# Top-32 attention with a following MLP: the selection of the limit for six row blocks at once, masks ten row blocks behind the scores

## The chip, the core and the metric

The kernel runs on one core of a Trainium2 chip. The metric is the device time of one launch in microseconds (us). A core has five engines with a queue each, which work through their own instructions in order and wait for one another by semaphores: PE (TensorE, matrix products), ACT (ScalarE), DVE (VectorE), POOL (GpSimd) and SP (SyncE, which issues most of the DMAs here).

## The reference

Attention over 64 heads (8 batches of 8), each with 576 rows of 64 numbers; of each row's 576 scores only those count that reach the 32nd largest. Then an MLP with a leaky ReLU over all 4608 tokens.

```python
scores = scale * np.matmul(q, k.transpose(0, 1, 3, 2))
kth = np.partition(scores, -top_k, axis=-1)[..., -top_k:-top_k + 1]
scores = np.where(scores >= kth, scores, -1000000000.0)
attn = np.exp(scores - np.max(scores, axis=-1, keepdims=True))
attn = attn / (np.sum(attn, axis=-1, keepdims=True) + 1e-09)
attn_out = np.matmul(attn, v)
# x: attn_out as 4608 tokens of 512
h = x @ w_in
out = (np.maximum(h, 0.0) + alpha * np.minimum(h, 0.0)) @ w_out
```

## The kernel before

**Row blocks.** Two heads make a pair; there are 32 pairs with nine row blocks (128 rows of one head, or the last 64 rows of both) each, 288 in all. `ORDER` lists them: pair after pair for the first 252, and mixed across the four pairs of the last batch for the last 36, so that its tokens become complete one group after another. One pass of the main loop (line 765) is a **tick**; in tick `n` the row block `n` gets its scores read, and older row blocks get their later steps. The order of instructions within each engine is written out by hand (`manual_schedule`), so the program's order is the engines' order.

**One row block's way.** PE computes the scores into PSUM (`scores`, line 326), one or two row blocks ahead. ACT copies them to `b` while adding `NT0`, the negative of an estimate of the row's limit (`act_b`, line 335), and sums the signs of `b` (`act_s`, line 341), which tells how many scores lie above the estimate. POOL makes of it a sign word `SG` (`side_of`, line 351), DVE turns the bits of `b` so that the scores on the wanted side of the estimate are ordered (`flip`, line 357, output `y`). DVE then finds the eight largest of each of six segments (`seg_ops`, line 367) two ticks behind the scores and merges the 48 candidates to the 24 largest, `L` (`merge_ops`, lines 382 and 384), three ticks behind. The place of the limit in this list is known from the sum of signs:

- `sel_a` (ACT, line 390): `ra = (S + 513)^2`
- `sel_eq` (DVE, line 395): `EQ` is one where `ra` equals an entry of the table `iota`, 24 entries per row block
- `sel_pr` (DVE, line 401): `L = EQ * L`
- `sel_sum` (DVE, line 405): the sum over the 24 entries, into `KK`
- `limit` (DVE, line 411): `KP`, the limit with its bits turned back

These five run once for three row blocks. Seven ticks behind the scores DVE compares `b` with the limit (`mask`, line 431, output `mk`), and POOL multiplies the mask with the exponentials (`weights`, line 441, output `w`). For the last six row blocks one fused DVE operation does both (line 438). The exponentials `e` come from ACT (`act_e`, line 346). SP transposes `w` by DMA (lines 449 to 454), and `tail_of` enters what follows in a calendar by ticks: the product with V on PE three or four ticks later (`av`, line 489; `av_last` for the last batch), the normalisation on DVE and ACT, the transposed tokens (`x_turn`), and the MLP's steps (`feed`).

**Units.** ACT handles `b` and `e` in units of one or two row blocks (`unit_of`). Row blocks 0 to 7 of a pair are four units of two; row block 8 is a unit by itself. A unit of two has five buffers for `b` and four for `e`, a unit of one has one of each. `act_e` comes in the tick of the unit's last row block.

**Prologue of a pair.** `prep_plan` prepares each pair (transposes of q and k, and the estimate `NT0` from a few statistics) in steps at fixed ticks relative to `BASE[p]`. `load` and `load_v` issue the loads of q, k and V some 18 and 13 ticks ahead of it; V lands in one of two buffers `st_v` and is copied to bf16 by ACT (`act_v`, line 201). From pair 12 on, and again from pair 21 on, the preparation runs one pair further ahead; the pairs 11 and 20 are prepared four ticks early for this.

**The MLP between.** The steps of the MLP (`ph_step`, line 644, with the ReLU `gT` on ACT, line 650; `pz_step`, lines 658 and 662, with a copy on ACT, line 667) and first the preparation of its weights (lines 556 to 620) wait in the queue `back`. Each tick has a credit of 1.9 (2.4 after the last scores), each step a price (0.9 for `ph`, 1.5 for `pz`). Up to tick 253 a tick takes one step at most, later as many as the credit allows with two banks at most.

**Order on DVE in a tick:** masks due, the sum of the selection held over from the tick before, the segments and merges interleaved, calendar steps `dve`, `limit`, `sel_eq`, `flip`, calendar steps `dvx`, `sel_pr`. On POOL: the products, then `SG`. On ACT: the ReLUs left from the tick before, `act_b` if a unit begins, calendar steps, `act_s`, `act_e` if a unit ends, `sel_a`.

Of the kernel before, what the change touches and what calls it, by code (L numbers as in the profile page):

```python
# [16 lines left out]
S = 576  # L17
NSEG = 6
SEG = S // NSEG
KW = 24  # L20
# [12 lines left out]
def kernel(  # L33
# [75 lines left out]
    st_vs = [prep.tile([128, 10, D], FP32, name=f"st_v{i}", bufs=1) for i in range(2)]  # L109
# [5 lines left out]
    def early_sets():  # L115
# [4 lines left out]
        for t_ in st_vs:  # L120
            nc.vector.memset(t_[64:128, 4, :], 0.0)
            nc.vector.memset(t_[0:64, 5, :], 0.0)
# [9 lines left out]
    def load(p, eng2=None):  # L132
# [10 lines left out]
        pairs[p] = dict(q=st_q, k=st_k, st_v=st_vs[p % 2], v=v_bfs[p % NV])  # L143

    def load_v(p):
        hA = 2 * p
        st_v = st_vs[p % 2]
# [14 lines left out]
    while n < NT:  # L162
        m = 1 if ORDER[n][1] == 8 and ORDER[n + 1][1] != 8 else 2
        for i in range(m):
            unit_of[n + i] = (n, m, i)
        units.append((n, m))
        n += m
    LEAD1, LEAD2 = 11, 20
    BASE = {p: TPP * (p - (p > LEAD1) - (p > LEAD2)) for p in range(NPAIR)}
    BASE[LEAD1] -= 4  # L170
    BASE[LEAD2] -= 4

    def prep_plan(p):
# [26 lines left out]
        def act_v():  # L200
            nc.scalar.copy(d["v"][:, :, 0:D], d["st_v"])
# [87 lines left out]
        if p == 1:  # L289
            ts = [-9, -8, -7, -6, -5, -4, -3, -2, -2, -2, -2, -2, -1, -1, 1]  # L290
        else:
            ts = [-14, -13, -12, -11, -10, -9, -7, -6, -5, -5, -4, -4, -3, -2, -8]
# [5 lines left out]
                 dict(dve=[dve_6]), dict(act=[act_v])]  # L298
# [29 lines left out]
    def act_b(n0):  # L328
        m = unit_of[n0][1]
        b = attn.tile([128, m, S], FP32, name=f"b{m}", bufs=5 if m == 2 else 1)  # L330
# [6 lines left out]
        tiles[n0]["bu"] = b  # L337
# [5 lines left out]
    def act_e(n0):  # L343
        m = unit_of[n0][1]
        e = attn.tile([128, m, S], BF16, name=f"e{m}", bufs=4 if m == 2 else 1)
        nc.scalar.activation(e, tiles[n0]["bu"], AF.Exp, scale=scl)  # L346
# [25 lines left out]

    def merge_ops(n):
        C = Cs[n // TPP][:, n % TPP, :, :].rearrange("p g e -> p (g e)")
        if n % 3 == 0:
            Ls[n // 3] = attn.tile([128, 3, KW], FP32, name="L", bufs=2)
        L = Ls[n // 3][:, n % 3, :]
# [10 lines left out]
    def sel_a(m):  # L388
        a = attn.tile([128, 3], FP32, name="ra", bufs=2)
        nc.scalar.activation(a, S_all[:, 3 * m:3 * m + 3], AF.Square, bias=c513)  # L390
        sel[m] = a

    def sel_eq(m):
        EQ = attn.tile([128, 3, KW], FP32, name="EQ", bufs=1)
        nc.vector.tensor_tensor(EQ, sel[m].unsqueeze(2).to_broadcast([128, 3, KW]),
                                iota.unsqueeze(1).to_broadcast([128, 3, KW]), ALU.is_equal)
        sel[m] = EQ

    def sel_pr(m):
        L = Ls.pop(m)  # L400
# [591 lines left out]
```

## Time and profile before

| | |
|---|---|
| median of three runs | 879.25 us |
| lowest and highest | 878.42 and 879.33 us |
| the profiled execution | 875.27 us |
| its span, first to last instruction | 873.2 us |
| mean granted TensorE clock | 0.919 |

The span is what the views below count from; the execution's own time is 2.1 us longer. A row of a group gives the line, the engine, the operation, output and inputs, the shapes, the count, the busy time in us, the mean duration in ns, and the idle time of the engine just ahead of it with what ended most of it. A row of the timeline gives start and duration in us. Durations of neighbours on an engine overlap in the records: the next instruction's start is earlier than the end of the one before. A row of a stretch gives the length and then the busy time of PE, PEld, DVE, ACT and POOL with counts, the granted clock, the DMA share and GB/s.

### The profile page before, as it was taken

The numbers are of one execution on the slowest core, as the hardware profiler recorded it, in microseconds if no ns is written. First come the engines' busy times: TensorE is split into PE (matmuls) and PEld (weight loads), VectorE is DVE, ScalarE is ACT, GpSimd is POOL, SyncE is SP. The second block draws the span as 40 slices with busy tenths as digits, with TensorE's granted clock in tenths as the row PEclk, the third lists the DMA queues.
The fourth block names the chain that finished last, engine by engine and source line by source line (L and its number), as shares of the span: only waits on it lengthen the run. The fifth ranks groups of instructions, "written<-read, shape, count | busy, mean of one in ns | idle before, by whom it ended". The sixth has DMA issues, their size and how long they took to land.

```text
span 873.2 us, 20627 instructions
## 1 busy us (share of the span) xinstructions
PE 725.9 (83%) x5747; PEld 426.9 (49%) x5747; DVE 833.7 (95%) x5185; ACT 789.7 (90%) x1873; POOL 430.1 (49%) x629
## 2 busy tenths in 40 slices
PE   6677687878968799878997789977897989899995
PEld 4344454434544355544454345634455555556663
DVE  4999999999999999999999999999999999999990
ACT  6999999899999999899998999999999999879851
POOL 1455455555545555545555554555554555555520
PEclk9666789699989999899987999999999999899998
DMA  7899644644666445555576456465456564355451
GB/s 163 154 180 204 122 96 92 128 95 88 147 129 116 90 109 120 114 117 95 118 159 116 83 104 132 104 129 101 101 118 123 112 101 100 80 96 101 81 99 41
DMA packets 343019, 99.50 MB, mean 114 GB/s; under 512 B 335200, under 2 KB 335216, under 8 KB 342896
## 3 DMA queue, kind: packets, MB, share of 16 engines
q1 hardware_dynamic: 340544, 95.71, 55.0%
q0 software_dynamic: 1152, 2.10, 1.9%
q8 instruction: 47, 0.77, 0.4%
q14 instruction: 76, 0.62, 0.3%
q10 hardware_dynamic: 1200, 0.30, 0.2%
HBM read 36.71 MB, written 9.44 MB: 53 GB/s over the span
## 4 chain that ended last, share of the span: by engine, by line
DVE 70%; ACT 13%; PE 12%; DMA 2%; issue 1%; POOL 1%; SPq 0%; DVEq 0%
DVE C L367 23%; DVE y L357 11%; DVE mk L431 10%; DVE C L384 9%; DVE L L382 8%; PE pz L662 3%; PE ps L326 3%; ACT b L335 3%; ACT h L341 3%; ACT e L346 2%; PE ph L644 2%; DVE P L244 2%; ACT gT L650 1%; DVE L L401 1%; DVE KK L405 1%
## 5 line engine op out<-in xcount | busy, mean ns | idle before, releaser
L441 POOL TENSOR_TENSOR w<-mk,e 128x576 bf16<-128x576 bf16 x250 | 318.9, 1276 | 336.5 <-DVE mk L431 183.9
L367 DVE MAX8 C<-y 128x8 f32<-128x96 f32 x1728 | 420.8, 244 | 0.1
L326 PE MATMUL ps<-qkT 64*128 64x288 f32 (+1 forms) x1280 | 253.8, 471 | 36.1 <-ACT b L335 35.9
L341 ACT ACTIVATE h<-b 128x576 bf16<-128x576 f32 x288 | 202.8, 704 | 1.6
L335 ACT ACTIVATE b<-ps,NT 128x576 f32<-128x576 f32 x288 | 202.0, 759 | 2.2 <-PE ps L326 2.1
L644 PE MATMUL ph<-xT,w_in_b 128*128 128x128 bf16 (+2 forms) x1088 | 158.5, 294 | 42.2 <-ACT gT L650 35.2
L326 PEld LDWEIGHTS ps<-qkT 64*128 64x128 f32 (+1 forms) x1280 | 133.6, 192 | 96.4 <-ACT b L335 60.1
L346 ACT ACTIVATE e<-b 128x1152 bf16<-128x1152 f32 (+1 forms) x158 | 174.1, 1102 | 0.0
L382 DVE MAX8 L<-C 128x8 f32<-128x48 f32 x864 | 163.5, 189 | 0.1
L357 DVE TENSOR_SCALAR y<-b,SG 128x576 int32<-128x576 int32 x288 | 147.1, 511 | 7.2 <-POOL SG L351 6.8
L431 DVE TENSOR_SCALAR mk<-b,KP 128x576 bf16<-128x576 f32 x282 | 143.8, 510 | 0.0
L644 PEld LDWEIGHTS <-w_in_b 128*128 128x128 bf16 x1088 | 85.7, 101 | 108.5 <-issue 80.0
L662 PE MATMUL pz<-w_out_b,gT 128*128 128x512 bf16 x576 | 138.6, 380 | 0.0
L650 ACT ACTIVATE gT<-ph 128x512 bf16<-128x512 f32 x144 | 88.0, 618 | 37.8 <-PE ph L644 37.6
L384 DVE MATCH_REPLACE8 C<-L,C 128x48 f32<-128x48 f32 x576 | 108.9, 189 | 0.0
L662 PEld LDWEIGHTS <-gT 128*128 128x128 bf16 x576 | 53.2, 98 | 70.6 <-issue 14.0
L489 PE MATMUL pu<-v_bf,wT 128*128 128x65 bf16 (+1 forms) x1600 | 69.6, 198 | 10.4 <-DMA wT<-w 6.8
L489 PEld LDWEIGHTS <-wT 128*128 128x128 bf16 (+1 forms) x1600 | 65.0, 103 | 21.4 <-DMA wT<-w 8.1
L351 POOL TENSOR_SCALAR SG<-S_all 128x1 int32<-128x1 f32 x288 | 64.6, 224 | 17.6 <-ACT h L341 17.5
L441 POOL TENSOR_TENSOR wm<-mk,e 128x576 bf16<-128x576 bf16 x32 | 40.8, 1275 | 49.9 <-DVE mk L431 47.1
L341 ACT ACTIVATION_READ_ACCUMULATOR h<-b 128x1 f32 x288 | 62.6, 217 | 0.0
L518 ACT ACTIVATE xb<-pu,rz 128x64 bf16<-128x64 f32 x224 | 54.3, 367 | 0.0
(100 smaller groups left out, 711.8 us busy)
## 6 DMA issues: line engine op xcount, KB each, us to landing
out_dram<-o_sb SPq DMA_DIRECT2D x35, 256.0 KB, 2.4
st_q<-in_q_dram SPq DMA_DIRECT2D x64, 128.0 KB, 2.9
st_v<-in_v_dram SPq DMA_DIRECT2D x64, 128.0 KB, 2.6
kst<-in_k_dram SPq DMA_DIRECT2D x62, 128.0 KB, 2.7
w_stage<-in_moe_w_out_dram SPq DMA_DIRECT2D x16, 256.0 KB, 3.1
w_in_b<-in_moe_w_in_dram POOLq DMA_DIRECT2D x8, 256.0 KB, 6.2
wT<-w SPq DMA_TRANSPOSE x128, 3.3
st_q<-in_q_dram SPq DMA_DIRECT2D x32, 32.0 KB, 2.7
```

The costliest lines, as they stand in the source:

```text
L326: nc.tensor.matmul(o_, l_, r_, start=True, stop=True)
L335: nc.scalar.activation(t["b"].rearrange("p (a c) -> p a c", a=2), t["ps"], AF.Identity, bias=NT0[:, p * TPP + j:p * TPP + j + 1], scale=ON ...
L341: nc.scalar.activation(h, tiles[n]["b"], AF.Sign, accum_out=S_all[:, n:n + 1])
L346: nc.scalar.activation(e, tiles[n0]["bu"], AF.Exp, scale=scl)
L357: nc.vector.tensor_scalar(t["y"].bitcast(I32), t["b"].bitcast(I32), FLIP, SG[:, n:n + 1], ALU.bitwise_xor, ALU.bitwise_xor)
L367: return [lambda g=g: nc.vector.max(out=C[:, n % TPP, g, :], in_=t["y"][:, g * SEG:(g + 1) * SEG]) for g in range(NSEG)]
L382: ops.append(lambda r=r, src=src: nc.vector.max(out=L[:, 8 * r:8 * r + 8], in_=src))
L384: ops.append(lambda r=r, src=src: nc.vector.match_replace(out=C2, in_to_replace=L[:, 8 * r:8 * r + 8], in_values=src, imm_value=NEG))
L431: nc.vector.tensor_scalar(t["mk"], t["b"], row_limit(n), None, ALU.is_ge)
L441: nc.gpsimd.tensor_tensor(dst, t["mk"], t["e"], ALU.mult)
L644: nc.tensor.matmul(hold[f][:, i, :], w_in_b[:, kk, (f + i) * 128:(f + i + 1) * 128], xT[:, kk, c0:c0 + tb], start=(kk == 0), stop=(kk == N ...
L662: nc.tensor.matmul(pz[0:m], hold["gT"][:, f, r0:r0 + m], w_out_b[:, f, :], start=False, stop=(f == NFT - 1))
```

## The change

- **Selection.** `GROUPS` forms groups of six for the first 252 row blocks and of three for the last 36. `sel_a`, `sel_eq`, `sel_pr`, `sel_sum` and `limit` run once for each group, their tiles are six wide.
- **Masks.** `mask` and `weights` of a row block come ten ticks behind its scores instead of seven; from row block 249 on this falls to seven, so that two row blocks fall due in each of the ticks 258, 259 and 260. Only the first of two gets a mask and the product on POOL; the second is done by the fused operation on DVE.
- **Exponentials.** `act_e` comes three ticks after its unit's last row block, two from row block 260 on, one from 268 on, none from 276 on.
- **Units.** Row blocks 0 to 7 are four units of two, row block 8 is a unit by itself, and from 9 on row blocks go two by two, across pairs; the last one is by itself. `b` has six buffers of two, `e` four of two.
- **Loads.** One buffer `st_v` instead of two; `load_v(1)` comes in tick 1, `act_v` of pair 1 in tick 5; `load_v(p)` not earlier than seven ticks ahead of `BASE[p - 1]`.
- **Preparation.** The pairs 11 and 20 are two ticks early instead of four, their followers two and one ticks late; `dve_6` moves to tick -3 behind `flip`.

```diff
-        m = 1 if ORDER[n][1] == 8 and ORDER[n + 1][1] != 8 else 2
+        m = 1 if n in (8, NT - 1) else 2
...
-    BASE[LEAD1] -= 4
-    BASE[LEAD2] -= 4
+    for p in (LEAD1, LEAD2):
+        for i, late in enumerate((-2, 2, 1)):
+            BASE[p + i] += late
...
-            ts = [-9, -8, -7, -6, -5, -4, -3, -2, -2, -2, -2, -2, -1, -1, 1]
+            ts = [-9, -8, -7, -6, -5, -4, -3, -2, -2, -2, -2, -2, -1, -1, -4]
         else:
-            ts = [-14, -13, -12, -11, -10, -9, -7, -6, -5, -5, -4, -4, -3, -2, -8]
+            ts = [-14, -13, -12, -11, -10, -9, -7, -6, -5, -5, -4, -4, -3, -3, -8]
...
-        b = attn.tile([128, m, S], FP32, name=f"b{m}", bufs=5 if m == 2 else 1)
+        b = attn.tile([128, 2, S], FP32, name="b", bufs=6)
...
-        e = attn.tile([128, m, S], BF16, name=f"e{m}", bufs=4 if m == 2 else 1)
-        nc.scalar.activation(e, tiles[n0]["bu"], AF.Exp, scale=scl)
+        e = attn.tile([128, 2, S], BF16, name="e", bufs=4)
+        nc.scalar.activation(e[:, 0:m, :], tiles[n0]["bu"], AF.Exp, scale=scl)
...
+    GROUPS = [(i, 6) for i in range(0, N0, 6)] + [(i, 3) for i in range(N0, NT, 3)]
+    group_of = {i: (g, z) for g, z in GROUPS for i in range(g, g + z)}
...
-    def sel_eq(m):
-        EQ = attn.tile([128, 3, KW], FP32, name="EQ", bufs=1)
-        nc.vector.tensor_tensor(EQ, sel[m].unsqueeze(2).to_broadcast([128, 3, KW]),
-                                iota.unsqueeze(1).to_broadcast([128, 3, KW]), ALU.is_equal)
-        sel[m] = EQ
+    def sel_eq(g, z):
+        EQ = attn.tile([128, 6, KW], FP32, name="EQ", bufs=1)[:, 0:z, :]
+        nc.vector.tensor_tensor(EQ, sel[g].unsqueeze(2).to_broadcast([128, z, KW]),
+                                iota.unsqueeze(1).to_broadcast([128, z, KW]), ALU.is_equal)
+        sel[g] = EQ
...
-            wdue.setdefault(wn + LAG_W if wn < NW else 3 * (wn // 3) + 7, []).append(wn)
+            g, z = group_of[wn]
+            at = wn + 10 - max(0, min(3, (wn - N0 + 5) // 2)) if wn < NW else g + 7
+            assert at >= g + z + 4
+            wdue.setdefault(at, []).append(wn)
+        edue = {}
+        for n0, m in units:
+            at = n0 + m - 1
+            edue.setdefault(at + (0 if at >= NT - 12 else 1 if at >= NT - 20
+                                  else 2 if at >= NT - 28 else 3), []).append(n0)
+        ga = {g + z: (g, z) for g, z in GROUPS}
+        gm = {g + z - 1: (g, z) for g, z in GROUPS}
...
+            if n == 1:
+                load_v(1)
...
-                if n == max(0, BASE[p] - 13):
+                if n == max(BASE[p] - 13, BASE[p - 1] - 7 + 4 * (p == 2)):
                     load_v(p)
...
-            if n >= 3 and n % 3 == 0 and n - 3 < NT:
-                sel_a((n - 3) // 3)
+            for n0 in edue.get(n, ()):
+                act_e(n0)
+            if n in ga:
+                sel_a(*ga[n])
...
-            for wn in due:
+            for wn in due[0:1]:
                 if wn < NW:
                     mask(wn)
...
-                weights(wn, wn >= NW)
+                weights(wn, wn >= NW or wn != due[0])
```

More of the change, by code (lines that the diff above doesn't have):

```diff
@@ L108 @@
     ksts = [prep.tile([128, 5, 130], FP32, name=f"kst{i}", bufs=1) for i in range(2)]
-    st_vs = [prep.tile([128, 10, D], FP32, name=f"st_v{i}", bufs=1) for i in range(2)]
+    st_v = prep.tile([128, 10, D], FP32, name="st_v", bufs=1)
     NV = 6
@@ L200, in act_v @@
         def act_v():
-            nc.scalar.copy(d["v"][:, :, 0:D], d["st_v"])
+            nc.scalar.copy(d["v"][:, :, 0:D], st_v)
         def pe_k():
@@ L297, in prep_plan @@
                  {dvx: [dve_3]}, dict(dve=[dve_4]), {dvx: [dve_4b]}, dict(dve=[dve_5]),
[L298 removed]
+                 {dvx: [dve_6]}, dict(act=[act_v])]
         if p == 0:
@@ L751 @@
         load_v(0)
-        load_v(1)
         for t in range(-16, 0):
@@ L835 @@
             run(n, "dve")
-            if 0 <= lm < NT and lm % 3 == 0:
-                limit(lm // 3)
+            if lm:
+                limit(*lm)
             if pick and n < NT:
-                sel_eq(mn // 3)
+                sel_eq(*pick)
             if 0 <= n - 1 < NT:
```

83 lines of the change are left out of this document (38 added, 45 removed).

## The prediction

> **What bounds the kernel now.** I read the page first: the share of each engine over the span, then the chain that ended last.
>
> ```profile
> span 873.2 us, 20627 instructions
> PE 725.9 (83%) x5747; PEld 426.9 (49%) x5747; DVE 833.7 (95%) x5185; ACT 789.7 (90%) x1873; POOL 430.1 (49%) x629
> DVE 70%; ACT 13%; PE 12%; DMA 2%; issue 1%; POOL 1%; SPq 0%; DVEq 0%
> ```
>
> VectorE (DVE) is busy 95% of the span and is 70% of the chain. A share over the whole span hides stages, so next the busy time by stretch: the middle, which the selection fills, and the tail.
>
> ```profile
> 100.00:740.00 640.00, 539.35 (x4244) 307.15 (x4243) 639.92 (x3993) 605.30 (x1475) 334.49 (x472) 0.95 0.56 111
> 800.00:850.00 50.00, 49.85 (x535) 32.92 (x534) 49.04 (x278) 37.25 (x74) 20.28 (x28) 1.00 0.47 93
> ```
>
> After the length stand PE, PEld, DVE, ACT, POOL. From 100 to 740 us DVE has 0.08 us free in 640, so each DVE nanosecond removed there shortens the kernel, as long as nobody makes DVE wait. ACT is next with 605.3 us, 34.7 us free. In the tail PE is as full as DVE. The middle has 223 masks, so a tick (one row block) takes 640 / 223 = 2.87 us.
>
> **The sum: the selection.** It is four DVE groups and one on ACT, once per three row blocks:
>
> ```profile
> L401 DVE TENSOR_TENSOR L<-EQ,L 128x72 f32<-128x72 f32 x96 | 21.3, 222 | 0.0
> L405 DVE TENSOR_REDUCE KK<-L 128x3 f32<-128x72 f32 x96 | 20.8, 216 | 0.1
> L395 DVE TENSOR_TENSOR EQ<-ra,iota 128x72 f32<-128x72 f32 x96 | 19.7, 206 | 0.0
> L411 DVE SCALAR_TENSOR_TENSOR KP<-KK,SG 128x3 int32<-128x3 int32 x96 | 13.8, 144 | 0.0
> L390 ACT ACTIVATE ra<-S_all,c 128x3 f32<-128x3 f32 x96 | 30.6, 319 | 0.0
> ```
>
> The 252 row blocks ahead of the last batch go from 84 calls to 42; the last 36 keep their 12 calls of three. A mean duration isn't what an instruction costs a full engine: the records overlap. The timeline's starts show the cost:
>
> ```profile
> 405.94 0.21 DVE L395 TENSOR_TENSOR EQ<-ra,iota 128x72 f32<-128x72 f32 x1
> 406.07 0.51 DVE L357 TENSOR_SCALAR y<-b,SG 128x576 int32<-128x576 int32 x1
> 406.50 0.22 DVE L401 TENSOR_TENSOR L<-EQ,L 128x72 f32<-128x72 f32 x1
> 406.65 0.51 DVE L431 TENSOR_SCALAR mk<-b,KP 128x576 bf16<-128x576 f32 x1
> 407.08 0.21 DVE L405 TENSOR_REDUCE KK<-L 128x3 f32<-128x72 f32 x1
> 407.21 0.24 DVE L367 MAX8 C<-y 128x8 f32<-128x96 f32 x1
> 408.87 0.13 DVE L411 SCALAR_TENSOR_TENSOR KP<-KK,SG 128x3 int32<-128x3 int32 x1
> 408.93 0.50 DVE L357 TENSOR_SCALAR y<-b,SG 128x576 int32<-128x576 int32 x1
> ```
>
> From its start to the next one's, EQ takes 0.13, the product 0.15, the sum 0.13 and KP 0.06: 0.47 us a call, 0.94 for six row blocks. What 72 more elements cost I take from small cousins of the same operations:
>
> ```profile
> L279 DVE TENSOR_TENSOR t<-sq,t 128x9 f32<-128x9 f32 x32 | 5.1, 160 | 0.1
> L282 DVE TENSOR_REDUCE sq<-t 128x9 f32<-128x27 f32 x32 | 5.1, 158 | 0.1
> ```
>
> From 9 to 72 elements a product grows from 160 to 222 ns, 1.0 ns an element; from 27 to 72 a reduction grows from 158 to 216, 1.3 ns. So the larger call costs 0.47 + 0.07 + 0.07 + 0.09 = 0.70 us, and 0.24 us is saved per six row blocks: 42 x 0.24 = **10 us**. The ends: nothing, if the second 72 elements cost as much as a call; 42 x 0.47 = 20 us, if they were free. The rows stand close to the value taken. ACT loses 42 of the 0.32 us squarings.
>
> Were the engine held for each whole duration, a call would cost 0.22 + 0.22 + 0.21 + 0.14 = 0.79 us, the larger one 1.02, and 42 x 0.56 = 23 us would go; the rows are against it, as EQ lasts 0.21 us and its successor starts after 0.13. The Trainium skill ("VectorE: DVE Perf Modes", section "The DRAIN you can't avoid") states this rule: the next operation doesn't start before the pipe has emptied. By it the 23 us would be the forecast.
>
> **The masks and the fused blocks.** Masks move three ticks later, and each with its product on POOL, its transposes on SP, the matmuls L489 and the feeding of the MLP. Their number stays; three masks leave the first ticks and return in ticks 258 to 260, where two row blocks fall due. There the second block takes the fused form on DVE instead of a mask:
>
> ```profile
> L431 DVE TENSOR_SCALAR mk<-b,KP 128x576 bf16<-128x576 f32 x282 | 143.8, 510 | 0.0
> L438 DVE SCALAR_TENSOR_TENSOR w<-b,KP,e 128x576 bf16<-128x576 f32 x6 | 4.5, 808 | 0.0
> ```
>
> That is 0.3 us more for each, **+1 us** with one small copy. The unknown: the fused one now runs beside a POOL product, which no row shows; a full wait behind that product (1.28 us, rows below) would make it +4.8; a gain is excluded, since nothing leaves DVE. I take 1. The Trainium skill ("SBUF — State Buffer", section "SBUF: two separate sides") says that a DVE operation with two SBUF inputs and a GpSimd operation that reads SBUF exclude each other, and the first to start keeps the port. By it the +1 stands if the fused one starts first, and it is the +4.8 if the product does.
>
> **POOL behind the mask.** In a tick without extra DVE work another chain is as long as DVE's:
>
> ```profile
> 401.19 0.52 DVE L431 TENSOR_SCALAR mk<-b,KP 128x576 bf16<-128x576 f32 x1
> 401.79 1.28 POOL L441 TENSOR_TENSOR w<-mk,e 128x576 bf16<-128x576 bf16 x1 [1.99 <-DVE mk L431]
> 403.03 0.23 POOL L351 TENSOR_SCALAR SG<-S_all 128x1 int32<-128x1 f32 x1
> 403.29 0.52 DVE L357 TENSOR_SCALAR y<-b,SG 128x576 int32<-128x576 int32 x1
> ```
>
> Mask, product, sign, y: 403.29 - 401.19 = 2.10 us, and y starts 0.03 after SG ended. EQ (0.13) or the sum with KP (0.19) stood between mask and y in two ticks of three; half of these 168 ticks lose them. Where nothing else stands there, about 0.02 us of the gain is held back: 84 x 0.02 = 1.7 at most; with other work in two thirds of the ticks I take **+0.6**.
>
> **Buffers of b and e.** Here the change adds waits. A b is held until its mask, 11 ticks, and there are six; the new act_b waits for a mask one tick ahead of it, where it was three. An exponential, now in the tick of the next but one act_b, needs the e of eight rows back, released by POOL's product one tick earlier, where it was two. How far ahead is ACT?
>
> ```profile
> 394.89 0.52 DVE L431 TENSOR_SCALAR mk<-b,KP 128x576 bf16<-128x576 f32 x1
> 404.41 1.39 ACT L335 ACTIVATE b<-ps,NT 128x576 f32<-128x576 f32 x2
> 406.23 0.23 ACT L341 ACTIVATION_READ_ACCUMULATOR h<-b 128x1 f32 x1
> 407.63 1.23 ACT L346 ACTIVATE e<-b 128x1152 bf16<-128x1152 f32 x1
> 408.48 0.22 POOL L351 TENSOR_SCALAR SG<-S_all 128x1 int32<-128x1 f32 x1
> ```
>
> The b of row blocks 137 and 138 starts 9.0 us after its mask (row block 127) ended: two ticks less leaves 3.3. Its exponential starts 4.6 us after the product that freed its e (row block 129, POOL at 401.79): one tick less leaves 1.7. Their first sign sum is done 2.0 us before POOL takes it. Behind a waiting exponential on ACT stand the next sign sum, gT and the following b, PE waits for gT, and DVE's y for the sign sum. So ACT will touch the buffers and lose part of its lead, but held at the limit it still has act_b one tick behind a mask and the sign sum wanted 2 x 2.87 us later. I take **0**; the other end is the rival below. Pairs across heads help ACT, which loses time behind a single row block (here ahead of row block 135); I count nothing for it while DVE is full:
>
> ```profile
> 398.52 0.60 ACT L650 ACTIVATE gT<-ph 128x512 bf16<-128x512 f32 x1 [1.48 <-PE ph L644]
> ```
>
> **Start.** One st_v instead of two: load_v(1) goes behind the loads of pair 2 and alpha on SP, and act_v(1) to tick 5; later each load of V waits for the copy three ticks or more before it, with ACT ahead of DVE. Exponentials leave ticks 1 and 3.
>
> ```profile
> 15.13 1.16 ACT L346 ACTIVATE e<-b 128x1152 bf16<-128x1152 f32 x1
> 18.99 1.29 POOL L579 DMA_DIRECT2D w_in_b<-in_moe_w_in_dram x2
> 20.59 0.52 DVE L357 TENSOR_SCALAR y<-b,SG 128x576 int32<-128x576 int32 x1 [2.39 <-POOL SG L351]
> ```
>
> DVE stands 2.39 us while POOL waits for alpha, which waits on ACT behind this exponential. Without it the chain moves up 1.06: **-1 us** (ends 0 and -2.4).
>
> **End.** Counting the queue of MLP steps tick by tick with the credits of the code: the block of rows 3456 is fed at tick 264 instead of 261, and the delay lasts. Four more steps (one of ph, three of pz) stand behind the last av_last, in ticks 295 and 296, which were empty.
>
> ```profile
> 839.11 3.62 PE L662 MATMUL pz<-w_out_b,gT 128*128 128x512 bf16 x16
> 842.63 1.96 PE L644 MATMUL ph<-xT,w_in_b 128*128 128x128 bf16 x32
> 853.06 0.49 PE L489 MATMUL pu<-v_bf,wT 128*128 128x65 bf16 x10 [0.33 <-DMA wT<-w]
> 857.24 5.55 PE L644 MATMUL ph<-xT,w_in_b 128*128 128x128 bf16 x64 [2.69 <-DMA xT<-xb]
> ```
>
> One ph step is 1.0 us, three of pz 1.0 + 3.6: 5.6 us, where PE now stands idle from 853.55 to 857.24. 5.6 - 3.7 = **+2 us** (ends 0 and +5.6).
>
> **Total:** -10 + 1 + 0.6 - 1 + 2 = -7.4. The profiled execution took 875.27 us (span 873.2); from that comes to 867.9. The three timed runs have a median of 879.25, 4 us above the profiled one; taken from this median, as it will be measured: **871.9 us**.
>
> **Rivals.**
> 1. *ACT becomes the bound* (slower). It has 34.7 / 223 = 0.16 us free per tick, and a DVE tick shortened by 0.04 leaves 0.12 (0.15 with the squarings gone). Should waits for b and e cost more than that, ACT sets the pace and its late sign sums stall y. The gain is gone at 0.19 us a tick; at 0.24, half a microsecond per pair, 240 ticks bring +12: 883. For it: the 1.7 us left above. Against: 2 us of lead at the other side, and ACT loses nothing to these buffers now. 9%.
> 2. *POOL's chain paces* (the change doesn't do what it says). Were every tick bare, only the product's part would remain, 42 x 0.07 = 3 us, less the 2.6 of the rest (1 + 0.6 - 1 + 2): 879. Against: the whole idle time ahead of y, the start included, is 7.2 us. 8%.
>
> ```profile
> L357 DVE TENSOR_SCALAR y<-b,SG 128x576 int32<-128x576 int32 x288 | 147.1, 511 | 7.2 <-POOL SG L351 6.8
> ```
>
> 3. *The end isn't hidden at all:* all 5.6 us behind the last block, 875. 13%.
> 4. *More stalls go:* the other 1.4 us of the third y's, the 1.0 that DVE has free from 800 to 850, and half of the 4.8 left ahead of y, since ACT with its exponentials put off comes sooner: 867. 12%.
> 5. *Whole durations count* (the drain): 858. 3%.
>
> My forecast, 871.9, has 55%. Its range with rivals 3 and 4 holds 80%: 865.5 to 877. A difference under 0.2% (1.8 us) can't be told from none here. Faster by more: 55 + 13 + 12 + 3 = 83%; within: 8%; slower: 9%.
>
> **What would show it.** The groups EQ, product and sum with 54 instructions, at some 280, 295 and 310 ns; DVE still without idle from 100 to 740; L438 with nine; y's start 0.03 after SG in more ticks; the stall of the third y shorter; PE busy up to the last ph. Wrong would be idle ahead of y released by SG with the sign sum just done (rival 1), or ACT idle ahead of e and b together with it.

## The result, and the profile after

| | before | after |
|---|---|---|
| median | 879.29 us (4 runs) | 922.85 us (4 runs) |
| lowest and highest | 878.42 and 880.8 | 920.76 and 924.37 |
| the profiled execution, its span | 875.27, 873.2 | 920.76, 919.0 |
| mean granted clock | 0.919 | 0.912 |

The kernel is slower by 4.9%: the ratio is 1.0492, with a 95% interval of 1.0465 to 1.0518. The forecast was 871.9 us, and 922.85 lies far outside its range.

The page of the kernel after, with the lines that answer to those of before (span, busy time by engine, chain that ended last by engine):

```profile
span 919.0 us, 20290 instructions
PE 740.4 (81%) x5677; PEld 421.4 (46%) x5747; DVE 837.0 (91%) x5016; ACT 784.4 (85%) x1818; POOL 428.4 (47%) x625
PE 26%; ACT 11%; DVE 5%; issue 1%; DMA 1%; SPq 1%; POOL 0%; ACTq 0%
```

In the chain DVE held 70% of the span and now holds 5%; PE leads it. (The shares of after add up to 45% of the span only, so this is a hint and no more.) The same stretch of the middle:

```profile
100.00:740.00 640.00, 517.08 (x3870) 283.95 (x3925) 605.06 (x3628) 564.09 (x1339) 316.10 (x445) 0.92 0.54 105
```

DVE is busy 605.06 of 640 us where it was busy 639.92. ACT, the suspect of the first rival, is less busy too (564.09 after 605.3). Every engine does less per microsecond, so the reason is waits and not work. The waits in this stretch (engine, line, waited for: us in total, times, longest), after and then before:

```profile
PE ph L648 <- ACT gT L654: 41.5, 47, 2.4
...
PE pr L235 <- DVE P L243: 30.6, 21, 3.7
ACT b L334 <- PE ps L325: 27.2, 19, 5.0
ACT gT L654 <- PE ph L648: 25.2, 30, 3.0
...
DVE rz L510 <- PE pu L493: 19.4, 24, 2.5
DVE y L356 <- POOL SG L350: 7.7, 14, 2.3
DVE P L243 <- PE pr L235: 7.3, 23, 0.4
```

```profile
PE ph L644 <- ACT gT L650: 34.5, 45, 1.5
ACT gT L650 <- PE ph L644: 22.8, 21, 2.7
PE pu L489 <- DVE P L244: 2.3, 3, 1.5
ACT b L335 <- PE ps L326: 0.4, 1, 0.4
```

DVE's three waits of after make 34.4 us, nearly all of the 34.9 that it lost (639.92 - 605.06). One line is new altogether: PE waits 30.6 us in `pr`, a step of a pair's preparation, for DVE's product `P` of the same preparation. No step of the prediction touched that wait.

The groups on DVE that the change made, by form (line, tiles, shapes, count, busy us, mean ns, idle before):

```profile
L404 DVE TENSOR_TENSOR L<-EQ,L 128x144 f32<-128x144 f32 x42 | 12.6, 299 | 0.0
L408 DVE TENSOR_REDUCE KK<-L 128x6 f32<-128x144 f32 x42 | 12.3, 294 | 0.0
L398 DVE TENSOR_TENSOR EQ<-ra,iota 128x144 f32<-128x144 f32 x42 | 11.9, 283 | 0.0
...
L442 DVE SCALAR_TENSOR_TENSOR w<-b,KP,e 128x576 bf16<-128x576 f32 x8 | 6.1, 806 | 0.0
L414 DVE SCALAR_TENSOR_TENSOR KP<-KK,SG 128x6 int32<-128x6 int32 x42 | 6.1, 146 | 0.0
...
L449 DVE COPY wm<-wm 128x64 bf16<-128x64 bf16 x1 | 1.1, 1142 | 0.0
```

The large selections take 283, 299 and 294 ns; 280, 295 and 310 were forecast. So the saving was sized well, and something else of some 50 us (922.85 less the forecast) came on top.

### Where it goes: two banks and three tiles

Two PSUM banks (the pool `ps_d` in the code above) serve the two products `pr` of a pair's preparation (one for the first 512 rows of both heads, one for the last 64), its statistics `st`, and the result `pu` of the product with V, which keeps its bank until ACT has read it. Which of them meet depends on the tick within the pair's cycle of nine. A pair's `pu` is computed three (first half) or four (second half) ticks behind its masks and released three later. With masks seven ticks behind the scores that is from tick 4 to 7 and from 1 to 4 of the cycle; `pr` comes in tick 8 and found both banks free. With masks ten ticks behind, the first `pu` holds a bank from tick 7 to tick 1, across tick 8. The second `pr` must then wait until DVE has read the first, at the end of DVE's next tick. PE in the timeline, after and then before:

```profile
418.82 0.41 PE L235 MATMUL pr<-qkT,GK 64*64 64x512 bf16 x2
420.38 0.22 PE L235 MATMUL pr<-qkT,GK 64*64 64x64 bf16 x2 [1.14 <-DVE P L243]
```

```profile
398.41 0.69 PE L236 MATMUL pr<-qkT,GK 64*64 64x512 bf16 x4
```

Before, the four matmuls stand in one row of 0.69 us. After, two and two stand apart, and between them lies DVE:

```profile
407.26 0.18 DVE L510 RECIPROCAL rz<-pu 128x4 f32<-128x4 f32 x1 [1.51 <-PE pu L493]
...
419.64 0.69 DVE L243 TENSOR_TENSOR P<-pr,qkT 128x512 bf16<-128x512 f32 x1
420.63 0.23 DVE L243 TENSOR_TENSOR P<-pr,qkT 128x64 bf16<-128x64 f32 x1 [0.31 <-PE pr L235]
```

The loss is not just the 1.14 us. PE runs ahead of DVE, and this lead lets it deliver `pu` before DVE asks (before, DVE didn't wait for it in this stretch). Once per pair it is now tied to DVE's place in the order; the lead is gone, and a later `pu` comes late. The 1.51 us of idle time on DVE at 407.26 belong to the pair before: its second `pr` started at 390.72 after a wait of 1.78 us. Between the two PE also waits 2.10 us for a ReLU, at 397.99, so this one place doesn't prove the chain; the experiments have to.

### The profile page after: what moved, and what is told of

Its sections match the earlier page's. It is cut to its first block, busy times and chain, and to the rows that moved or that the text cites. A ratio compares the mean times of both kernels' runs of the same rounds, so it can differ in the third digit from the quotient of the medians.

```text
span 919.0 us, 20290 instructions
## 1 busy us (share of the span) xinstructions
PE 740.4 (81%) x5677; PEld 421.4 (46%) x5747; DVE 837.0 (91%) x5016; ACT 784.4 (85%) x1818; POOL 428.4 (47%) x625
## 5 line engine op out<-in xcount | busy, mean ns | idle before, releaser
L325 PE MATMUL ps<-qkT 64*128 64x288 f32 (+1 forms) x1280 | 267.4, 481 | 15.9 <-ACT b L334 15.5
L334 ACT ACTIVATE b<-ps,NT 128x576 f32<-128x576 f32 x288 | 199.6, 753 | 36.1 <-PE ps L325 33.9
L648 PE MATMUL ph<-xT,w_in_b 128*128 128x128 bf16 (+2 forms) x1065 | 155.5, 289 | 53.8 <-ACT gT L654 46.9
L325 PEld LDWEIGHTS ps<-qkT 64*128 64x128 f32 (+1 forms) x1280 | 130.5, 196 | 108.3 <-issue 49.7
L345 ACT ACTIVATE e<-b 128x1152 bf16<-128x1152 f32 (+1 forms) x145 | 170.9, 1178 | 0.0
L385 DVE MAX8 L<-C 128x8 f32<-128x48 f32 x864 | 165.4, 191 | 0.1
L666 PE MATMUL pz<-w_out_b,gT 128*128 128x512 bf16 x562 | 136.5, 380 | 1.5 <-issue 1.1
L340 ACT ACTIVATION_READ_ACCUMULATOR h<-b 128x1 f32 x288 | 65.0, 226 | 0.0
L235 PE MATMUL pr<-qkT,GK 64*64 64x64 bf16 (+1 forms) x128 | 20.8, 330 | 46.9 <-DVE P L243 37.1
```

The source lines that it names most:

```text
L325: nc.tensor.matmul(o_, l_, r_, start=True, stop=True)
L334: nc.scalar.activation(t["b"].rearrange("p (a c) -> p a c", a=2), t["ps"], AF.Identity, bias=NT0[:, p * TPP + j:p * TPP + j + 1], scale=ON ...
L340: nc.scalar.activation(h, tiles[n]["b"], AF.Sign, accum_out=S_all[:, n:n + 1])
L345: nc.scalar.activation(e[:, 0:m, :], tiles[n0]["bu"], AF.Exp, scale=scl)
L385: ops.append(lambda r=r, src=src: nc.vector.max(out=L[:, 8 * r:8 * r + 8], in_=src))
L648: nc.tensor.matmul(hold[f][:, i, :], w_in_b[:, kk, (f + i) * 128:(f + i + 1) * 128], xT[:, kk, c0:c0 + tb], start=(kk == 0), stop=(kk == N ...
```

## The experiments

Theory A: the banks. Theory B, the first rival of the prediction: ACT's buffers for `b` and `e`. Theory C came up when A left a remainder: the tick in which an exponential stands. All times are medians; ratios are to the kernel before timed beside each (879.3 to 880.8 us), with their 95% interval.

| kernel | us | ratio |
|---|---|---|
| after | 922.85 | 1.0492 [1.0465, 1.0518] |
| after, even distances | 909.09 | 1.0345 [1.0308, 1.0382] |
| after, own bank | 894.23 | 1.0164 [1.0111, 1.0217] |
| both | 881.42 | 1.0008 [0.9984, 1.0032] |
| both, own bank from pair 3 | 877.92 | 0.9981 [0.9961, 1.0002] |
| the same, later feed | **875.18** | **0.9949 [0.9929, 0.9969]** |

### The banks

**The second `pr` in another pool.**

```diff
+            if nm == "pr1" and p not in (0, LEAD1, LEAD2):
+                pool, tag = ps_a, "pa"
```

> The changed kernel with one edit: the second part of the estimate's product (pr1) gets the PSUM bank of ps_a, which stands free then, instead of one of the two banks of ps_d. Theory A (the banks: with the masks three ticks later a pu holds one of the two banks of ps_d while pr0 and pr1 are computed, so PE waits at pr1 for DVE's first P, loses its lead once a pair, and DVE waits for PE): the gap between pr0 and pr1 goes back from 1.2 to 4.3 us to 0.25 to 0.43 us, the waits of PE at pr for DVE's P (37 us in the changed kernel) go, and the time is 866 to 877 us. Theory B (the buffers of b and e hold ACT back, which then makes DVE wait): the time stays at 915 to 923 us, since these buffers are as before.

Measured: 894.23 us, ratio 1.0164 [1.0111, 1.0217]: 28.6 us less than after. That lies between the two forecasts: theory B's is refuted, and theory A's 866 to 877 us is missed by 17. In the waits from 100 to 740 us PE's wait in `pr` for `P` is gone and DVE's waits shrink, but not to nothing:

```profile
DVE rz L512 <- PE pu L495: 12.7, 17, 2.1
DVE y L358 <- POOL SG L352: 0.6, 3, 0.2
```

**The same edit in the kernel before**, as a control.

> The kernel before with only the bank of pr1 changed in the same way. Control: in the kernel before no pu stands in ps_d while pr0 and pr1 are computed, so by theory A nothing changes (877 to 881 us); if the bank is worth something by itself, it is faster by several us, and the first run's gain isn't a repair of what the change did.

Measured: 882.43 us, ratio 1.002 [0.9997, 1.0043]. The edit by itself brings nothing.

**The kernel before with one bank for both `pr`.** This puts the suspected wait, alone, into the kernel before.

```diff
+            if nm in ("pr0", "pr1") and p not in (0, LEAD1, LEAD2):
+                pool, tag = ps_a, "pa"
```

> The kernel before with only this edit: pr0 and pr1 of a pair go one after the other through the single bank of ps_a, so that PE has to wait at pr1 until DVE has read pr0, as in the changed kernel. Masks, exponentials, units, buffers and groups are as before. Theory A: 905 to 925 us, with gaps between pr0 and pr1 of one us and more, and DVE waiting for pu and P. Theory B: 877 to 883 us.

Measured: 904.66 us, ratio 1.0288 [1.0245, 1.0332], 24 us slower, just under theory A's range. The wait that was put in, from 100 to 740 us:

```profile
PE pr L238 <- DVE P L246: 34.4, 24, 3.3
```

The wait is like that of the kernel after (30.6 us, 21 times), and the price of 24 us is near the 28.6 that came back. So the bank is shown from both sides, and it isn't the whole loss.

### The selection by itself

**Own bank, and groups of three throughout.**

```diff
-    GROUPS = [(i, 6) for i in range(0, N0, 6)] + [(i, 3) for i in range(N0, NT, 3)]
+    GROUPS = [(i, 3) for i in range(0, NT, 3)]
```

> The same edit as in the first run, and the selection in groups of three for all 288 row blocks; masks, exponentials, units and loads as in the changed kernel. It shows what the larger groups are worth by themselves. By starts in the traces a call of six costs 0.71 us and two calls of three 0.95, so 10 us over 42 groups: this run is 8 to 11 us slower than the first. If POOL's chain from the mask to y paces DVE, it is 0 to 3 us slower.

Measured: 900.94 us, ratio 1.0237 [1.0209, 1.0265]. The groups of six are worth 6.7 us between the medians and 9.8 between the spans (899.7 and 889.9) of two kernels that both wait; 8 to 11 were expected. How a large call stands on DVE, in the kernel with its own bank:

```profile
523.83 0.18 DVE L512 RECIPROCAL rz<-pu 128x4 f32<-128x4 f32 x1 [0.95 <-PE pu L495]
...
523.99 0.28 DVE L400 TENSOR_TENSOR EQ<-ra,iota 128x144 f32<-128x144 f32 x1
524.19 0.51 DVE L358 TENSOR_SCALAR y<-b,SG 128x576 int32<-128x576 int32 x1
...
524.69 0.29 DVE L406 TENSOR_TENSOR L<-EQ,L 128x144 f32<-128x144 f32 x1
524.91 0.51 DVE L437 TENSOR_SCALAR mk<-b,KP 128x576 bf16<-128x576 f32 x1
```

From start to start: EQ 0.20, the product 0.22. With 0.21 for the sum and 0.07 for KP (medians over the 42 calls) that is 0.70 us, the forecast.

### The tick of the exponentials

With its own bank the kernel still took 14 us more than the kernel before (880.45 us beside it), though its selection is cheaper. In its timeline, ACT (first four rows) and PE (last):

```profile
513.21 0.65 ACT L656 ACTIVATE gT<-ph 128x512 bf16<-128x512 f32 x1
513.69 1.44 ACT L336 ACTIVATE b<-ps,NT 128x576 f32<-128x576 f32 x2
...
516.23 1.24 ACT L347 ACTIVATE e<-b 128x1152 bf16<-128x1152 f32 x1
517.28 0.67 ACT L656 ACTIVATE gT<-ph 128x512 bf16<-128x512 f32 x1
...
518.00 1.02 PE L650 MATMUL ph<-xT,w_in_b 128*128 128x512 bf16 x4 [1.59 <-ACT gT L656]
```

A unit of two gives ACT its two `b` in the tick of the first row block. Units follow each other every two ticks, so the distance decides: at three ticks the exponential, which counts for two ticks as well, falls into the tick of the next unit's two `b`. That tick holds two `b`, a sign sum and an exponential, the other one only a sign sum, beside the ReLUs and calendar steps. The ReLU `gT` behind it starts 4.07 us after the one before, PE with one bank for `ph` stands 1.59 us, and its lead is spent.

**Even distances: four, two and none instead of three, two, one and none** (with the own bank).

```diff
-            edue.setdefault(at + (0 if at >= NT - 12 else 1 if at >= NT - 20
-                                  else 2 if at >= NT - 28 else 3), []).append(n0)
+            edue.setdefault(at + (0 if at >= NT - 12 else 2 if at >= NT - 28 else 4),
+                            []).append(n0)
```

> The changed kernel with pr1 in its own bank (first run) and one more edit: exponentials come four ticks after their unit's last row block instead of three (two from row block 260 on, none from 276 on), so that an exponential stands in the tick between two act_b and not in the tick of an act_b. Theory C (the rest of the loss, 14 us over the kernel before and some 22 over what the selection should give: ACT's ticks are now unequal, with two b, a sign sum and an exponential in one and one sign sum in the next; gT at the head of a tick comes late behind the exponential, PE waits for it with the next ph, then has the short tick to do its work, and DVE waits for pu): 872 to 884 us, with less than 30 us of PE's waits for gT at ph (52 in the first run) and less than 8 us of DVE's waits for pu (18). Theory D (the products with V, now in other ticks of a pair beside the transposes of q and the Gram matrix, make PE late whatever ACT does): 890 to 897 us.

Measured: 881.42 us, ratio 1.0008 [0.9984, 1.0032], 12.8 us less. Over the whole run DVE's waits for `pu` at line 512 fall from 18.0 to 7.5 us, below the 8 that theory C forecast; PE's waits for `gT` fall from 52 to 41.3 only, where it forecast less than 30. Its ACT: the exponentials stand in the other tick. From 506 to 524 us the ReLUs come every 2.4 to 3.5 us, where with three ticks they came after 1.7 to 1.9 and 3.6 to 4.1 us by turns (506 to 523 us).

```profile
509.33 0.67 ACT L656 ACTIVATE gT<-ph 128x512 bf16<-128x512 f32 x1
...
510.47 1.25 ACT L347 ACTIVATE e<-b 128x1152 bf16<-128x1152 f32 x1
...
511.71 0.68 ACT L656 ACTIVATE gT<-ph 128x512 bf16<-128x512 f32 x1
512.19 1.46 ACT L336 ACTIVATE b<-ps,NT 128x576 f32<-128x576 f32 x2
...
514.27 0.73 ACT L656 ACTIVATE gT<-ph 128x512 bf16<-128x512 f32 x1
```

**Five, three, one and none** (odd, but still later; own bank), against the line of the kernel after:

```diff
+            edue.setdefault(at + (0 if at >= NT - 12 else 1 if at >= NT - 20
+                                  else 3 if at >= NT - 28 else 5), []).append(n0)
```

> The same with exponentials five ticks after their unit's last row block (three from row block 260 on, one from 268 on, none from 276 on): later than in the 881 us run, but with an odd distance. Parity theory: 888 to 900 us. Delay theory: 881 us or less.

Measured: 896.19 us, ratio 1.0158 [1.0114, 1.0202], as with three. So being later isn't what helps.

**Two and none** (even, but earlier; own bank):

```diff
+            edue.setdefault(at + (0 if at >= NT - 12 else 2), []).append(n0)
```

> The changed kernel with pr1 in its own bank and exponentials two ticks after their unit's last row block (none from row block 276 on), instead of three there and four in the run that came to 881 us. Parity theory (what costs is that an exponential stands in the tick of an act_b; with units of one fixed parity, two by two across pairs, this makes every second tick of ACT long, while in the kernel before the single row blocks shift the parity from pair to pair): an even distance again, 878 to 888 us. Delay theory (what helped was one more tick of distance): 894 us or more, since the exponentials come earlier.

Measured: 896.13 us, ratio 1.0158 [1.0127, 1.0189]. The parity theory's 878 to 888 us are missed, so "even" isn't the whole rule. Here theory B's mechanism, a wait for a buffer, appears in size. The waits from 100 to 740 us:

```profile
ACT e L347 <- POOL w L447: 19.8, 32, 1.5
...
ACT e L347 <- POOL wm L453: 4.9, 4, 2.0
```

An exponential two ticks behind needs one of the four buffers of `e` before POOL has given it back. At four ticks these lines are not there, and they are not in the kernel after either. No run gave `e` more buffers, so that they make up the 15 us is likely and not shown.

**The kernel after with even distances, banks as they are**, to see whether the two causes add up (the edit of the even distances above, alone).

> The changed kernel with only the exponentials at +4 (two from row block 260 on), pr1 in the bank of the changed kernel. It completes the square of the two repairs: 923 with neither, 894 with the bank, 881 with both. If the two losses are independent, 906 to 913 us; if the wait at pr1 alone holds PE back whatever ACT's ticks look like, 918 to 923 us.

Measured: 909.09 us, ratio 1.0345 [1.0308, 1.0382]. Of the four corners (923, 909, 894, 881) the bank is worth 28.6 and 27.7 us, the distance 13.8 and 12.8. They add up.

**The exponentials one tick later in the kernel before**, up to the last batch.

```diff
+            edue.setdefault(at + (0 if at >= N0 else 1), []).append(u0)
...
-                        act_e(n0)
...
+            for u0 in edue.get(n, ()):
+                act_e(u0)
```

> The kernel before with one edit: up to the last batch the exponential comes one tick later, so that it stands in the tick of the following act_b. Masks, groups, units, banks and buffers are as before. Theory C: 885 to 900 us, with more waits of PE for gT and DVE waiting for pu or for SG. Theory D: 877 to 883 us.

Measured: 878.26 us, ratio 0.9978 [0.995, 1.0006]. An odd distance alone is harmless there, against theory C's forecast. But in the kernel before row block 8 is a unit by itself, so the parity changes with every pair. Hence two more:

**Units two by two across pairs in the kernel before**, alone, and with the odd distance.

```diff
-        m = 1 if ORDER[n][1] == 8 and ORDER[n + 1][1] != 8 else 2
+        m = 1 if n in (8, NT - 1) else 2
```

> The kernel before with one edit: units two by two across pairs, exponentials in the tick of the unit's last row block as before. Parity theory: 874 to 881 us, since ticks stay equal; ACT and PE lose the stop behind each single row block, DVE stays the bound.

> The kernel before with exponentials one tick later (as in the run that came to 878 us) and with row blocks in units two by two across pairs; masks seven behind, groups of three, five and four buffers as before. Parity theory: now the parity is fixed and every second tick is long, 886 to 900 us. If the distance of masks is needed for the loss: 875 to 882 us.

Measured: 882.64 us, ratio 1.0036 [1.0006, 1.0065], alone; 892.95 us, ratio 1.0127 [1.0099, 1.0156], with the odd distance. So it takes both parts of the change: the units fix the parity, and the distance puts it on the wrong side. Together they cost 14.7 us over the odd distance alone and 10.3 over the units alone. (The units alone came out 1.6 us above their forecast.) So theory C is shown in this form: an exponential in the tick of `act_b` costs 10 to 15 us when the units fix the parity.

### The rest: where the selection's 10 us stay

With both causes undone the kernel was as fast as before, though its selection is cheaper. Five runs looked for the remainder.

**Selections of three and masks seven ticks behind for the first 12 row blocks, and the mask instead of the fused operation for a row block 8 that falls due with another** (on the kernel with both causes undone).

```diff
-    GROUPS = [(i, 6) for i in range(0, N0, 6)] + [(i, 3) for i in range(N0, NT, 3)]
+    GROUPS = [(i, 3) for i in range(0, 12, 3)] + [(i, 6) for i in range(12, N0, 6)]
+    GROUPS += [(i, 3) for i in range(N0, NT, 3)]
...
+            if wn < 12:
+                at = wn + 7
...
+        for due in wdue.values():
+            if len(due) == 2:
+                due.sort(key=lambda wn: ORDER[wn][1] != 8)
```

> The 881 us version (pr1 in its own bank, exponentials at +4) with two more edits. First, the first twelve row blocks keep groups of three and masks seven ticks behind: in the 881 us version a b of the row blocks 11 to 18 reuses a buffer that is released by a mask of its own tick, because the single row block 8 takes a whole buffer, and DVE stands 3 us for a late pair soon after. Second, of two row blocks that fall due in one tick, one with j = 8 gets the mask and POOL's product and the other the fused operation, which saves the copy of 1.1 us that stood beside POOL's product. Expected 875 to 879 us: 2 to 3 us at the start, 1 at ticks 258 to 260, and 0.5 lost for two more calls of the selection. If the start isn't held by these buffers: 879 to 881.

Measured: 882.71 us, ratio 1.0042 [1.0024, 1.0061], no gain. Both edits did what they were meant to: the stall of 2.76 us, at 63.78 us in the kernel with both causes undone, is not in this trace, and neither is the copy of 1.14 us. But DVE stands later instead, 1.19 us at 70.70 and longer at 90.68:

```profile
90.68 0.18 DVE L513 RECIPROCAL rz<-pu 128x4 f32<-128x4 f32 x1 [3.26 <-PE pu L496]
```

**Masks and POOL products in place of the fused operations.** What the fused ones cost, from the kernel after (DVE, then POOL):

```profile
798.29 0.80 DVE L442 SCALAR_TENSOR_TENSOR wm<-b,KP,e 128x576 bf16<-128x576 f32 x1
799.13 1.14 DVE L449 COPY wm<-wm 128x64 bf16<-128x64 bf16 x1
...
788.90 1.28 POOL L445 TENSOR_TENSOR w<-mk,e 128x576 bf16<-128x576 bf16 x1 [1.27 <-issue]
...
798.50 1.72 POOL L445 TENSOR_TENSOR w<-mk,e 128x576 bf16<-128x576 bf16 x1 [1.54 <-issue]
```

The product beside the fused operation lasts 1.72 us instead of 1.28, and the small copy ends at 800.27, just after the product (800.22). So the product waits for the fused operation, which started 0.21 us earlier, and the copy for the product. The Trainium skill ("SBUF — State Buffer", section "SBUF: two separate sides") calls the shared port pair an exclusive lock that whichever starts first keeps for its whole instruction. The trace agrees for the fused operation: it takes 0.80 us, no longer than alone. Three fused operations and the copy take 3.35 us from start to start in the kernel with both causes undone (0.73, 0.84 and 0.73, and 1.06 for the copy); before, three masks were in their place elsewhere (3 x 0.43).

```diff
-            for wn in due[0:1]:
+            for wn in due:
...
-                weights(wn, wn >= NW or wn != due[0])
+                weights(wn, wn >= NW)
```

> The kernel with its own bank for pr1 and even distances for the exponentials (881.4 us), and the second row block of the ticks 258 to 260 gets a mask on DVE and its product on POOL like all others, with two buffers for the mask. Theory (the fused blocks beside POOL's product are dear): by the starts on DVE the two fused blocks and the copy of 128x64 took 3.35 us more than before and masks for these three blocks would take 3 x 0.43 = 1.3, so some 2.5 to 3.5 us go: 878 to 879. Rival (POOL with two products in a tick is late with the sign words, so the time returns as idle ahead of y): within 1 us of 881.4, with idle ahead of y released by SG between 775 and 800 us.

Measured: 881.57 us, ratio 1.003 [1.0009, 1.0051]. The rival was right about the time: POOL has two products in one tick, the sign word comes late, and DVE waits for that, though at 756 to 761 us and not from 775 on.

```profile
761.15 0.52 DVE L358 TENSOR_SCALAR y<-b,SG 128x576 int32<-128x576 int32 x1 [1.21 <-POOL SG L352]
```

From 740 to 800 us these waits make 1.7 us, after 0.3 with the fused operations, and that takes back most of the 2.1 us (3.35 less 1.29) that the masks save. Two row blocks in one tick are dear either way.

**The own bank only from pair 3 on.** The experiments' own edit had made a wait at the start, seen on PE of the kernel with even distances:

```profile
24.83 1.12 PE L196 MATMUL pq<-ident_f,st_q 128*128 128x128 f32 x4 [1.97 <-DVE P L245]
```

```diff
-            if nm == "pr1" and p not in (0, LEAD1, LEAD2):
+            if nm == "pr1" and p not in (0, 1, 2, LEAD1, LEAD2):
```

> The same kernel (881.4 us), with pr1 in the other pool only from pair 3 on. Theory (that edit itself makes a wait at the start: PE stands 1.97 us at 24.8 us with pq of pair 2 behind DVE's product of pair 1, and the stall of 3.05 us at 32.3 follows from it): the wait at 24.8 goes and the stall at 32.3 falls to about 2.5 as in the kernel after, perhaps the one at 63.8 (2.76) with it; 878 to 881. Rival (the stalls at the start come from ACT and the half clock there, as they stand in the kernel after too): within 1 us of 881.4, with both stalls as they were.

Measured: 877.92 us, ratio 0.9981 [0.9961, 1.0002]. DVE's stall near 32 us, which stands behind the preparation, fell from 3.04 to 1.42 us, the one near 63 us stayed. Against the version with both causes undone that is 3.5 us by the medians and 2.4 by the ratios, but the two were not timed together, their intervals overlap, and the spans of their profiled executions are alike (876.3 and 876.2).

**Both of these edits.**

> Both edits of the two runs beside it. Theory: they lie in different stretches and add up, 875 to 879, below the kernel before (879.3). Rival: what one of them saves is lost again at a later wait, and it is no faster than the better one alone.

Measured: 881.07 us, ratio 1.0014 [0.999, 1.0037]. They don't add up, as the rival had it: beside the bank from pair 3 on, the masks in place of the fused operations cost 3.2 us, and beside those masks the later bank brings only 0.5.

**Two ticks more for one block of tokens.** In the kernel with its own bank from pair 3 on, PE stands once for a long time, and DVE waits for `pu` after it (PE's timeline, then DVE's only wait from 657 to 752 us):

```profile
664.17 1.89 PE L650 MATMUL ph<-xT,w_in_b 128*128 128x256 bf16 x8 [5.13 <-DMA xT<-xb]
...
DVE rz L512 <- PE pu L495: 5.5, 7, 1.2
```

The MLP's step on these tokens is in PE's queue before the DMA has turned them. By the code the edit enters one block later, the rows 2816 to 3071:

```diff
-                        put(n + 8, "end", lambda: feed(b * S + 256))
+                        put(n + (10 if b == 5 else 8), "end", lambda: feed(b * S + 256))
```

> The kernel with its own bank from pair 3 on and even distances (877.9 us), and the MLP's steps for the rows 2560 to 3136 entered two ticks later. Theory (PE's one wait of 5.13 us at 664 us, for the transposed tokens, costs PE the lead, and the seven waits for pu after it, 5.5 us on DVE between 657 and 752 us, follow from it): the wait at 664 goes and most of the 5.5 us with it, 873 to 876. Rival (the waits for pu there come from the pairs 25 to 27 themselves, whose steps stand closer): they stay, 877 to 879.

Measured: 875.18 us, ratio 0.9949 [0.9929, 0.9969]. The stretch from 657 to 752 us, first without and then with the edit:

```profile
657.00:752.00 95.00, 79.49 (x667) 49.89 (x673) 89.50 (x538) 82.05 (x193) 46.62 (x67) 0.93 0.49 100
```

```profile
657.00:752.00 95.00, 82.65 (x695) 50.45 (x696) 94.97 (x565) 85.08 (x200) 50.82 (x71) 0.96 0.53 104
```

DVE is full again (94.97 of 95 us). Moving one step on PE by two ticks returned 5.5 us of DVE's time in this stretch; the kernel as a whole gained 2.7 us by the medians. This version, three small edits to the kernel after, is faster than both kernels; against the one before it gains 0.5%.

## Why the prediction was wrong

**The bound** was read rightly: DVE is full in the middle and PE and ACT have time to spare. What was missed is what this rests on. DVE is full only because PE and ACT are early, and the change moved steps that keep them early. The prediction's own clause, "as long as nobody makes DVE wait", was examined for buffers of ACT and for POOL's chain, and not for PE.

**Selection, -10 us:** right in mechanism and size (0.70 us for a large call). The rival by which whole durations count is refuted: start to start EQ takes 0.20 us and lasts 0.28. The section of the Trainium skill that the prediction names for this rival ("VectorE: DVE Perf Modes", "The DRAIN you can't avoid") also says that a next operation that isn't held starts earlier, which the prediction left out. These starts agree with that, so by that section the 23 us were not to be forecast.

**Masks and fused blocks, +1 us: the step that failed.** It says that each mask moves "with its product on POOL, its transposes on SP, the matmuls L489 and the feeding of the MLP" and that "their number stays". The number does; but the matmuls L489 hold a bank, and three ticks later they hold it while `pr` needs it. That is 28 us. The feeding moved with them: PE's wait for the turned tokens of one block was 0.89 us in the kernel before, 2.75 in the kernel after, and 5.13 in the repaired one, where it cost DVE 5.5 us. Why it grew, although turning and feeding keep their distance in ticks, no run shows. The fused operations were sized rightly: 2.30 us from start to start, 1.0 more than three masks. The "one small copy", put at 0.1 us at most, took 1.06, because it stood behind POOL's product. So the term was 2.1 and not 1.

**POOL's chain, +0.6 us:** of no account. In the fastest version `y` waits 0.4 us for `SG` in the whole middle. The 7.7 us in the kernel after go together with ACT's 27.2 us of waiting for scores; with `pr` in its own bank 0.6 and 8.1 remain.

**Buffers of b and e, 0:** right for the kernel after, which has no wait of ACT for a mask or a product in the middle. With the causes undone ACT does touch the limit, as the step foresaw. In the fastest version, from 100 to 740 us:

```profile
ACT b L336 <- DVE mk L437: 8.2, 16, 1.0
```

That costs DVE little: it is busy 637.83 of those 640 us. The first rival had the sign and not the cause, and its price contradicts itself: if the gain is gone at 0.19 us a tick, 12 us more make 891 and not 883 (and with the squarings gone its rows leave 0.17 us a tick free, not 0.15). But the step looked at an exponential's new tick for its buffer alone, and that is the second step that failed: its neighbours on ACT cost 13 us. "I count nothing" for units across pairs was wrong too: alone they cost 0.36% [0.06, 0.65], and it is they that fix the parity.

**Start, -1 us:** `y` of the third row block comes 1.04 us earlier (19.55 after 20.59, its stall 1.34 after 2.39), as forecast, and it is soon lost: 2.54 us of idle time at 31.80, where DVE waits for ACT's part of the preparation, and the seventh `y` comes at 32.55 after 31.95. DVE doesn't bound this stretch. So the masks that left it saved nothing there and cost in full where they came back.

**End, +2 us:** not seen. From the last `y` to the end of the span it takes 919.0 - 884.47 = 34.53 us, and 873.2 - 838.73 = 34.47 before. The extra steps do stand there: from 884.4 to 904 us PE is busy 19.49 of 19.60 us, and before, from 838.7 to 857, 13.98 of 18.30. What the step left out is the clock. The last `ph`, 5.55 us in the prediction's row, ran at a granted clock of 0.66; now the clock is 1.00 and the row reads:

```profile
904.80 3.75 PE L648 MATMUL ph<-xT,w_in_b 128*128 128x128 bf16 x64 [0.74 <-DVE bad L483]
```

With these 1.8 us taken off, the step's 5.6 - 3.7 leaves 0.1.

**The sum of what the runs showed:** 28 for the bank and 13 for the distance are 41 of the 43.6 us. With both undone the kernel stood at the time of the kernel before, though the selection alone was worth 7 to 10 us. With the bank from pair 3 on and the later feed 4.7 us appear (875.18 against 879.85); what holds the rest is not shown, and replacing the fused operations returned nothing. Open stays a stall of 2.8 us near 62 us. The granted clock from 60 to 62 us is 0.50 there and 1.00 in the kernel before, but the kernel before with one bank has 0.50 as well and no stall; smaller selections and earlier masks at the start only exchanged it for a later one. Open is also how much of the 28 us is the wait itself and how much the lost lead.

## What to carry to other kernels

A step moved by some ticks takes along everything that it holds. List each bank and buffer in its pool with the ticks from first write to last read, modulo the cycle of the loop, and lay the lists of before and after side by side, above all for pools that several stages share. Do the same for the work of each tick on the engines that run ahead: a full engine stays full only while its suppliers keep their lead, and an evenly loaded supplier keeps it where an alternately loaded one with the same total doesn't.

## What the runs showed of the hardware

- A DVE operation with 72 elements more per partition (144 for 72) costs 0.07 us more from start to start (EQ 0.20 after 0.13, the product 0.22 after 0.15).
- A copy of 128x64 bf16 on DVE took 1.14 us beside a POOL product, and the product 1.72 instead of 1.28 us beside a fused operation with two inputs, which kept its 0.80 us.
- A wait of PE of up to 3.3 us, about once per pair, cost a kernel bound by DVE 24 us in all (the kernel before with one bank), though without it PE was busy only 539.35 of 640 us in the middle.
- The same 64 matmuls of `ph` at the end took 5.55 us at a granted clock of 0.66 and 3.75 us at 1.00.
